# An attention and token/channel-mixer kernel: plain loads and casts for the first q and k halves, all run-time masks on VectorE, gated v loads, and a listed order for the opening

## The chip, the cores and the metric

The kernel runs on one core of one Trainium2 chip. The metric is the device time of one execution in microseconds (us); lower is better. Engines are called PE (TensorE matmul), PEld (its weight loads), DVE (VectorE), ACT (ScalarE), POOL (GpSimd) and SP (SyncE, which here only issues DMAs).

## What is computed

Four batches of eight heads go through causal attention with a window of 128 positions and four sink positions; the result goes through a token mixer and a channel mixer. Cut to what matters, with B, H, S, D = 4, 8, 768, 64:

```python
scores = (q @ k.T) / sqrt(D)                       # per head, 768 x 768
keep   = (pos_k < 4) | ((0 <= pos_q - pos_k) & (pos_q - pos_k < 128))
a      = softmax(where(keep, scores, -1e9))
x      = (a @ v), heads side by side               # 4 x 768 x 512
h      = relu(x.T @ w_tok1) @ w_tok2               # w_tok1 768 x 256, w_tok2 256 x 768
u      = x + h.T
out    = u + relu(u @ w_ch1) @ w_ch2               # w_ch1 512 x 1536, w_ch2 1536 x 512
```

## The kernel before

Heads are taken in eight groups of four, two groups to a batch. Work is written as operations with names: a prefix, the group or batch, and an index. The names matter, because the change lists them.

Attention for group g: `Lq`, `Lk` load q and k as bf16; `Tq`, `Tk` turn them by 32x32 blocks on DVE (L354); `KZ` makes a block form of the four sink keys (L378). Scores are made transposed, keys on the partitions, and only where the window allows: key tile kt meets query tiles kt and kt+1. `SCg.u` covers key tiles 2u and 2u+1 (u = 0, 1, 2) for four heads (L406); groups 0 and 1 split it into two pairs of heads. `EX` takes the exponential from PSUM to SBUF as tile pT (ACT, L423). `MK` zeroes what the window excludes (below). `SK` and `EXK` do the sink scores (L476, L481). `PVg.qt` multiplies by v for one query tile (L495, L498, L503); v carries a column of ones, so the last column is the sum. `XB` divides by it into the batch's x (DVE, L518, L519). `Lv` loads v as float32 through SP (L335) and `Cv` casts it (L211 on DVE or L212 on POOL).

Mixer for batch b: `T1` (L547) and `H1` (relu), then `T2` (L599), `U` (add x, DVE L604), `X` (transposes, L609) and `UTE` (copies). Batch 0 makes part of this directly as `TT` (L578, L581) and `UE`. Then `C1` (L632) with its relu `V` (ACT L217 or DVE L219), `C2` in three parts (L654), `O` (residual add, DVE L664) and `ST` (store, SP L669). Weights `Wtok1`, `Wtok2`, four pieces `Wch1` and two `Wch2` are float32 in HBM and are cast by DMAs that POOL issues (L714), as are q and k (L325).

Masks before: DVE multiplies pT by a 0/1 tile for the first half of u = 0 (`MKg.0h`, 1024 elements per partition, L444). All other 128-wide blocks (512 elements over the four heads) are separate operations that may go to POOL as affine selects (L224, L229) or to DVE as multiplications (L437). For two score blocks, (1,1) and (1,2), PE adds a mask of large negative numbers before the exponential instead (L399, from tile `mneg`).

The order is decided when the program is built. `order_of` is a greedy list planner: each operation has a cost per engine, a priority and, for loads, a landing time; at each step it takes the operation that can start first, by priority and distance from the end within 0.2 us. Each engine then runs its own list strictly in order and waits for semaphores of the others. PSUM is planned as slots: two of kind `sc` (two banks each, scores) and four of kind `mx` (one bank each, everything else). Where the plan sees PE idle before 36 us, `Filler` puts dummy matmuls on a zero tile `warm` there (L754); they depend on the memset of `warm` alone (L233). The planner starts PE at 0.8 us and does not add that memset to a filler's start.

v loads: five of them stand at the head of SP's list and wait for nothing on other engines, since the raw tiles have five buffers. SP's plain loads and POOL's casting loads are two DMA queues.

Of the kernel before, what the change touches and what calls it, by code (L numbers as in the profile page):

```python
# [9 lines left out]
FP32 = mybir.dt.float32  # L10
# [4 lines left out]

INF = float("inf")


# [7 lines left out]
class Op:  # L26
# [4 lines left out]
    def __init__(self, name, engines, emit, deps=(), pri=0, rows=False, take=(), free=(), land=0.0, dear=None):  # L31
        self.name, self.engines, self.emit = name, engines, emit
        self.deps, self.pri, self.rows = [d for d in deps if d is not None], pri, rows
        self.take, self.free, self.land, self.dear = take, free, land, dear or {}
        self.dmas = 1 if land else 0
        self.far = 0.0
        self.begin = self.end = self.engine = None
        Op.n += 1
        self.seq = Op.n
# [11 lines left out]
def order_of(ops, slots, filler):  # L51

    free_at = {e: 0.8 for e in ("PE", "ACT", "DVE", "POOL", "SP")}
    banks = {kind: [0.0] * n for kind, n in slots.items()}
    dma_free, rows = 1.9, False
    flying = {"SP": [0.0] * 8, "POOL": [0.0] * 8}
# [21 lines left out]
    while waiting:  # L78
# [30 lines left out]
        if o.land:  # L109
            dma_free = max(dma_free, t + 1.2) + o.land  # L110
            o.end = dma_free + 0.9
            flying[e] += [o.end] * o.dmas
        else:
            o.end = free_at[e]
# [21 lines left out]
def kernel(  # L136
# [34 lines left out]
    singles = ctx.enter_context(tc.tile_pool(name="singles", bufs=1))  # L171
    stage = ctx.enter_context(tc.tile_pool(name="stage", bufs=5))
    bfp = ctx.enter_context(tc.tile_pool(name="bfp", bufs=2))
# [15 lines left out]
    mfirst = singles.tile([P, 2 * P], BF16, name="mfirst")  # L189
    mrest = singles.tile([P, 2 * P], BF16, name="mrest")  # L190
    mneg = singles.tile([P, 2, 4 * P], BF16, name="mneg")
# [113 lines left out]
    groups = [Group() for _ in range(NG)]  # L305
    PEM = ((1, 1), (1, 2))
    PIECES = (2, 1, 1, 1, 1, 1, 1, 1)
    PAIRS = (1,)
    V0, V0w = 1, "q"
    BW, BWV = 0.37, 0.25  # L310

    def load_ops(g, deps, vdeps, pri):

        G = groups[g]
        C = PIECES[g]
        R = S // Q // C
        G.bf, G.load = {}, {"q": [], "k": [], "v": []}
        prev = groups[g - 2] if g >= 2 else None
        pieces = [(w, c) for c in range(C) for w in "qk"]
        for n, (w, c) in enumerate(pieces):  # L320
            def emit(e, w=w, c=c):
                if w not in G.bf:
                    G.bf[w] = bfp.tile([P, S // Q, D], BF16, name=w + "b")
                src = heads(q if w == "q" else k, g)
                nc.gpsimd.dma_start(out=G.bf[w][:, ts(c, R)],  # L325
                                    in_=src.rearrange("h (i r) d -> (h i) r d", i=Q)[:, ts(c, R)])
            o = op(f"L{w}{g}.{c}", ("POOL", 0.8), emit, deps + (prev.dt[w] if prev else []), pri + n,
                   land=GH * S * D * 4e-6 / BW / C)
            G.load[w].append(o)
        parts = 2 if g == 1 else 1  # L330
        for x in range(parts):
            def vv(_, x=x, n=GH // parts):
                if "v" not in G.bf:
                    G.bf["v"] = stage.tile([P, GH * S * D // P], FP32, name="raw_v", tag="raw")
                nc.sync.dma_start(out=G.bf["v"].rearrange("p (n d) -> p n d", d=D)[:, ds(x * n * NT, n * NT)],  # L335
                                  in_=heads(v, g)[ds(x * n, n)].rearrange("h (t p) d -> p (h t) d", p=P))
            G.load["v"].append(op(f"Lv{g}.{x}", ("SP", 0.46), vv, vdeps, pri + 2, land=GH * S * D * 4e-6 / BWV / parts))


    def attention(g, xb, base):  # L340
# [31 lines left out]
        veng = {"POOL": 1.02e-3 * N}  # L372
        if g < 2:
            veng |= {"DVE": dve(N, 2), "ACT": act(N)}
        G.cv = [op(f"Cv{g}", veng, castv, G.load["v"] + [c_va_op] + old, -5 if g < 2 else base + 2)]
# [51 lines left out]
        def masks(u, ex):  # L427
            if (g, u) in PEM:
                return []
            n = 512 if u < 2 else 384  # L430

            def block(e, x, c):
                t = G.pT[u][:, :, ds(256 * x + P * c, P)]
                if e == "POOL":
                    (causal, behind)[c](nc.gpsimd, t, 0.0)
                else:
                    nc.vector.tensor_tensor(  # L437
                        out=t, in0=t, op=ALU.mult,
                        in1=mrest[:, ts(c, P)].rearrange("p (o x) -> p o x", o=1).to_broadcast([P, GH, P]))
            r, xs = [], [0, 1]  # L440
            if u == 0:
                def head(e):
                    t = G.pT[u][:, :, 0:2 * P]
                    nc.vector.tensor_tensor(  # L444
                        out=t, in0=t, op=ALU.mult,
                        in1=mfirst[:, 0:2 * P].rearrange("p (o x) -> p o x", o=1).to_broadcast([P, GH, 2 * P]))
                r = [op(f"MK{g}.0h", ("DVE", dve(1024, 2)), head, ex + [c_first_op], base + u)]
                xs = [1]
            for x in xs:
                for c in range(2 if 2 * u + x < NT - 1 else 1):  # L450
                    r.append(op(f"MK{g}.{u}{x}{c}", {"POOL": 0.76, "DVE": dve(512, 2) + 0.1}, lambda e, x=x, c=c: block(e, x, c),
                                ex + [c_rest_op], base + u, dear={"DVE": 0.6}))
            return r
# [248 lines left out]
    for o in groups[0].load["v"] + groups[1].load["v"]:  # L702
        o.deps += groups[V0].load[V0w][-1:]
    o_vsl = op("vsl", ("POOL", 2.6), c_vsink_load, [o_vs, groups[0].load["k"][1]], -150, land=0.2)
    o_vsl.dmas = 4
    c_vsink_op = op("vs1", ("POOL", 0.6), c_vsink_one, [o_vs, o_vsl], -60)
    o_first = op("first", ("POOL", 0.65), c_masks(mfirst), [o_ones], -120)
    c_first_op = op("first1", ("DVE", 0.17), c_mfirst_sink, [o_first], -120)
    c_rest_op = op("rest", ("POOL", 0.65), c_masks(mrest), [o_ones], -20)

    def weight(key, dst, src, deps, pri, run):

        def emit(e):
            nc.gpsimd.dma_start(out=dst, in_=src)  # L714
        w_ops[key] = op(f"W{key}", ("POOL", 0.8), emit, deps, pri, land=dst.shape[0] * dst.shape[1] / 16 * run * 1e-3)
        return w_ops[key]
# [14 lines left out]
    for b in range(B):  # L731
        batches[b].x = X(batches[b - 2].u if b >= 2 else [])
        for a in range(GB):
            g = GB * b + a
            if g >= 2:
                deps = [c1w[3]] if g < 4 else []
                load_ops(g, deps, deps + groups[g - 2].cv, 1000 * b - 700)
            attention(g, batches[b].x, 1000 * b + 10 * a)
        mixer(b, 1000 * b + 50, 1000 * b + 1100)
    for o in ops:  # L740
        if 0 <= o.pri < 60:
            o.pri = 0

    class Filler:
# [48 lines left out]
```

## Time and profile before

| what | value |
|---|---|
| median of 6 runs | 221.9 us (221.14 to 222.26) |
| the profiled execution's own time | 221.65 us |
| its span, first to last instruction | 219.7 us |
| what lies around the span | 1.95 us |
| mean granted TensorE clock | 0.999 |
| PE busy | 204.3 us, 93% of the span |
| DVE busy | 122.0 us, 56% |
| ACT busy | 104.3 us, 47% |
| POOL busy | 65.6 us, 30% |
| DMA | 23.10 MB, mean 105 GB/s |

PE is the busiest engine by far, so the table is read for where PE is not busy: the first 33 us, a stretch between 77 and 110 us, and the tail. In the timeline a line gives the start, the duration, the engine, the source line, the operation, its tiles, and in brackets the idle time of that engine just before and what ended it. In the chain of work that ended last, a line gives a start, a duration and what held the end of the kernel at that moment. A DMA's packets are counted in the bytes that they write, so a casting load of 384 KB has read 768 KB.

### The profile page before, as it was taken

What the parts mean: (1) busy time and instruction counts of PE and PEld (TensorE: products, weight loads), DVE (VectorE), ACT (ScalarE), POOL (GpSimd) and SP (SyncE); (2) the same over time, 40 slices, a digit from 0 to 9 for tenths busy, and PEclk for the clock granted to TensorE, in tenths of its full rate; (3) what the DMA queues carried; (4) which work ended last, traced back from release to release, by engine and by line L of the source; (5) the groups of instructions that cost most, each with busy time, mean ns of one, the idle gap of its engine ahead of it and who ended that gap; (6) DMA issues with size and microseconds to landing.
All of it is one profiled execution on the core that took longest, in us unless ns stands there. A gap on an engine that the chain in (4) does not pass through costs nothing.

```text
span 219.7 us, 4249 instructions
## 1 busy us (share of the span) xinstructions
PE 204.3 (93%) x1767; PEld 115.7 (53%) x1767; DVE 122.0 (56%) x222; ACT 104.3 (47%) x174; POOL 65.6 (30%) x105
## 2 busy tenths in 40 slices
PE   7976799999999967899999999999999999999993
PEld 3332486555545635467555554467655545655552
DVE  6769972091778999999994113578481122001131
ACT  2077516753347676684565330587553301753300
POOL 7919940006038889562020000146100000000000
PEclk9999999999999999999999999999999999999999
DMA  7999999998999898320000112200001112101122
GB/s 149 223 213 221 208 204 206 211 213 177 233 215 218 198 213 139 36 46 0 3 0 0 51 48 95 97 3 3 0 0 51 48 48 104 43 1 48 48 97 97
DMA packets 36243, 23.10 MB, mean 105 GB/s; under 512 B 26112, under 2 KB 31488, under 8 KB 36224
## 3 DMA queue, kind: packets, MB, share of 16 engines
q0 software_dynamic: 7904, 10.24, 27.8%
q1 hardware_dynamic: 28320, 12.59, 23.5%
q8 instruction: 14, 0.23, 0.4%
q14 instruction: 5, 0.04, 0.1%
HBM read 26.77 MB, written 6.29 MB: 150 GB/s over the span
## 4 chain that ended last, share of the span: by engine, by line
PE 77%; DMA 7%; DVE 6%; POOL 4%; ACT 2%; issue 1%; POOLq 0%; ACTq 0%
PE ps_v L632 29%; PE ps_w L654 28%; PE ps_u L599 5%; DMA w_tok<-in_moe_w_tok_dram 4%; PE ps_h L547 4%; DMA vsink<-in_v_dram 3%; PE ps_s L406 3%; PE ps_ut L609 2%; PE ps_o L498 2%; DVE kT L354 2%; PE ps_o L503 2%; PE ps_o L495 2%; ACT pT L423 1%; PE ps_k L476 1%; DVE pT L444 1%
## 5 line engine op out<-in xcount | busy, mean ns | idle before, releaser
L217 ACT ACTIVATE v<-ps_v 128x384 bf16<-128x384 f32 x90 | 44.2, 491 | 53.4 <-PE ps_v L632 42.2
L632 PE MATMUL ps_v<-uT,w_ch 128*128 128x384 bf16 x384 | 67.4, 326 | 0.2
L654 PE MATMUL ps_w<-w_ch,v 128*128 128x512 bf16 (+1 forms) x300 | 65.0, 371 | 0.0
L423 ACT ACTIVATE pT<-ps_s 128x1024 bf16<-128x1024 f32 (+1 forms) x48 | 43.3, 952 | 36.4 <-PE ps_s L406 33.9
L664 DVE TENSOR_TENSOR o<-ps_w,u_sb 128x512 f32<-128x512 f32 (+1 forms) x25 | 16.7, 669 | 67.6 <-PE ps_w L654 67.6
L632 PEld LDWEIGHTS <-w_ch 128*128 128x128 bf16 x384 | 36.5, 98 | 25.3 <-DVE x_b L519 0.6
L654 PEld LDWEIGHTS <-v 128*128 128x128 bf16 x300 | 29.1, 98 | 31.3 <-issue 0.2
L224 POOL TENSOR_SCALAR_AFFINE_SELECT pT<-pT 128x512 bf16<-128x512 bf16 x29 | 21.9, 761 | 54.6 <-issue 32.4
L604 DVE TENSOR_TENSOR u_sb<-ps_u,x_b 128x512 bf16<-128x512 f32 x24 | 15.3, 682 | 12.5 <-PE ps_u L599 12.4
L519 DVE TENSOR_TENSOR x_b<-ps_o,rc 128x256 bf16<-128x256 f32 (+1 forms) x45 | 19.9, 442 | 1.6
L406 PE MATMUL ps_s<-qT,kT 32*128 32x256 bf16 (+1 forms) x384 | 16.9, 263 | 2.6 <-ACT pT L423 1.1
L354 DVE STREAM_TRANSPOSE qT<-qb 128x768 uint32<-128x768 uint32 (+1 forms) x9 | 16.8, 1865 | 3.6 <-DMA qb<-in_q_dram 3.6
L498 PE MATMUL ps_o<-va,pT 128*128 128x65 bf16 x192 | 15.8, 194 | 1.6 <-DVE pT L444 1.0
L354 DVE STREAM_TRANSPOSE kT<-kb 128x768 uint32<-128x768 uint32 (+1 forms) x9 | 16.9, 1872 | 0.2
L498 PEld LDWEIGHTS <-pT 128*128 128x128 bf16 x192 | 13.5, 98 | 4.4 <-DVE pT L444 1.3
L406 PEld LDWEIGHTS <-kT 32*128 32x128 bf16 x384 | 9.4, 92 | 11.6 <-issue 7.8
L503 PE MATMUL ps_o<-va,pT 128*128 128x65 bf16 x160 | 14.8, 193 | 0.0
L547 PE MATMUL ps_h<-x_b,w_tok 128*128 128x256 bf16 x96 | 12.3, 273 | 1.6 <-DMA w_tok<-in_moe_w_tok_dram 1.3
L599 PE MATMUL ps_u<-h,w_tok 128*128 128x512 bf16 x48 | 12.5, 378 | 1.3 <-DVE u_sb L604 0.9
L229 POOL TENSOR_SCALAR_AFFINE_SELECT pT<-pT 128x512 bf16<-128x512 bf16 x19 | 12.9, 685 | 0.0
L754 PE MATMUL ps_warm<-warm 128*128 128x512 bf16 x43 | 11.3, 423 | 1.3 <-DVE warm L233 1.3
L325 POOL DMA_DIRECT2D qb<-in_q_dram x9 | 5.0, 558 | 24.1 <-DVE qT L354 21.9
(61 smaller groups left out, 159.1 us busy)
## 6 DMA issues: line engine op xcount, KB each, us to landing
out_dram<-o SPq DMA_DIRECT2D x23, 256.0 KB, 2.0
raw_v<-in_v_dram SPq DMA_DIRECT2D x7, 768.0 KB, 8.3
qb<-in_q_dram POOLq DMA_DIRECT2D x7, 384.0 KB, 6.6
kb<-in_k_dram POOLq DMA_DIRECT2D x7, 384.0 KB, 7.9
w_ch<-in_moe_w_ch_dram POOLq DMA_DIRECT2D x4, 384.0 KB, 11.1
w_ch<-in_moe_w_ch_dram POOLq DMA_DIRECT2D x1, 1024.0 KB, 15.3
raw_v<-in_v_dram SPq DMA_DIRECT2D x2, 384.0 KB, 14.5
w_tok<-in_moe_w_tok_dram POOLq DMA_DIRECT2D x2, 384.0 KB, 8.2
```

The lines of the kernel that those rows point to most:

```text
L217: nc.scalar.activation(o, i, AF.Relu)
L224: eng.affine_select(out=t, in_=t, compare_op=ALU.is_ge, fill=fill, base=0, pattern=[[0, t.shape[1]], [1, P]], channel_multiplier=-1)
L354: nc.vector.transpose(G.T[w].rearrange("p s x -> p (s x)").bitcast(UINT32).rearrange("p (i r) -> p r i", i=Q)[:, r], G.bf[w][:, r].bitcast ...
L406: nc.tensor.matmul(bank[h][:, at:at + w], G.T["k"][r, ts(kt, P), db], G.T["q"][r, ds(kt * P, w), db], start=not pem and db == 0, stop=db = ...
L423: nc.scalar.activation(o, i, AF.Exp, scale=scale)
L498: nc.tensor.matmul(ps[:, h], G.pT[qt // 2][:, h, ds(256 * (qt % 2), P)], G.va[:, h, qt], start=(qt < 2 and h == 0), stop=(h == GH - 1 and ...
L503: nc.tensor.matmul(ps[:, h], G.pT[kt // 2][:, h, ds(256 * (kt % 2) + P, P)], G.va[:, h, kt], start=False, stop=(h == GH - 1), skip_group_c ...
L519: nc.vector.tensor_tensor(out=xb.tile[:, ds(q0, n), c0:c0 + W].rearrange("p n (h d) -> p n h d", h=GH), in0=ps[:, :, :, 0:D], in1=rc.to_br ...
L547: nc.tensor.matmul(p.tile, w_tok1[:, t, ts(tt, P)], xb.tile[:, t, ds(a * W, W)], start=(t == 0), stop=(t == NT - 1))
L599: nc.tensor.matmul(ps, w_tok2[:, tt, ts(st, P)], M.h1t[:, tt], start=(tt == 0), stop=(tt == NTOK - 1))
L632: nc.tensor.matmul(ps, w_ch1[:, c, ts(ft, P)], M.uT[hf][:, c], start=(c == 0), stop=(c == NC - 1))
L654: nc.tensor.matmul(p.tile, M.v1t[hf][:, ft, ts(st % NH, P)], w_ch2[:, ft, ds(lo, n)], start=(ft == 0), stop=(ft == NF - 1))
```

## The change

- For group 0 the first halves of q and k are loaded as float32 by SP (two plain DMAs at the head of its list, ahead of the v loads) and cast: k's by DVE, q's by ACT. The other halves and all later q and k stay with POOL.
- POOL takes no masks at run time. `MK` is now on DVE alone, in larger pieces: for u = 0 two of 1024 elements (the mask tiles `mfirst` and `mrest`), for u = 1 one of 2048, for u = 2 one of 1536. `mrest` becomes 512 wide. Of the two blocks masked on PE only (1,2) stays; (1,1) becomes a DVE piece. The cast `Cv` of every group is now POOL's.
- The raw v tiles have three buffers instead of five, and the load of v for groups 2 and 3 carries a wait on one of the `Wch1` weight pieces, so what stands behind it on SP waits too.
- The planner counts the landing of SP's and POOL's DMAs apart and with other delays.
- A list `FIRST` gives the order and the engine of some 160 operations of groups 0 and 1 and of batch 0's first mixer part. Among other things it puts the memset of `vsink` (2080 elements, 1.8 us) ahead of that of `warm` on DVE, moves `mneg`'s selects on POOL behind the sink loads `vsl`, puts `Cv0` ahead of the weight DMAs and `Cv1` behind the first two, and takes the third score block of groups 0 and 1 first.
- After the opening the planner makes another order too. In the built program PE's scores of groups 4 and 5 now stand among `C1` of batch 1; before, those of groups 2 to 5 all stood among `C2` of batch 0 and the start of batch 1. PE has 38 fillers ahead of its first score instead of 35, and two more sets of three later.

The diff, cut to its core:

```diff
+FIRST = """
+MK0.00:D UE0.03:A PV1.3:P vs1:G XB0.1:D SK1:P C10.03:P C10.02:P Tq0.1:D Lv0.0:S Tk1.0:D PV1.5:P XB1.2:D
...
+"""
-    dma_free, rows = 1.9, False
+    dma_free, rows = {"SP": 1.9, "POOL": 3.4, "ACT": 1.9}, False
...
-            dma_free = max(dma_free, t + 1.2) + o.land
-            o.end = dma_free + 0.9
+            dma_free[e] = max(dma_free[e], t + (2.5 if e == "POOL" else 1.4)) + o.land
+            o.end = dma_free[e] + 0.9
...
-    stage = ctx.enter_context(tc.tile_pool(name="stage", bufs=5))
+    stage = ctx.enter_context(tc.tile_pool(name="stage", bufs=3))
...
-    mrest = singles.tile([P, 2 * P], BF16, name="mrest")
+    mrest = singles.tile([P, 4 * P], BF16, name="mrest")
...
-    PEM = ((1, 1), (1, 2))
+    PEM = ((1, 2),)
...
+            if g == 0 and c == 0:
+                def plain(e, w=w, src=src):
+                    raws[w] = stage.tile([P, R, D], FP32, name="raw_" + w, bufs=1)
+                    nc.sync.dma_start(out=raws[w], in_=src)
+
+                def cast(e, w=w, bf=bf):
+                    copy_on[e](bf(), raws[w])
+                o = op(f"L{w}{g}.{c}", ("SP", 0.46), plain, [], pri + n, land=land)
+                o = op(f"C{w}{g}.{c}", {"ACT": act(R * D), "DVE": dve(R * D, 2)}, cast, [o], pri)
+            else:
+                def casting(e, src=src, bf=bf):
+                    nc.gpsimd.dma_start(out=bf(), in_=src)
...
+                if gate:
+                    behind_of(ins, gate)
...
         veng = {"POOL": 1.02e-3 * N}
-        if g < 2:
-            veng |= {"DVE": dve(N, 2), "ACT": act(N)}
...
-            n = 512 if u < 2 else 384
-
-            def block(e, x, c):
...
+            for lo, hi, m in ((0, 256, mfirst), (256, 512, mrest)) if u == 0 else ((0, 512 if u == 1 else 384, mrest),):
+                def mask(e, lo=lo, hi=hi, m=m):
+                    t = G.pT[u][:, :, lo:hi]
+                    nc.vector.tensor_tensor(out=t, in0=t, op=ALU.mult,
+                                            in1=m[:, 0:hi - lo].rearrange("p (o x) -> p o x", o=1).to_broadcast([P, GH, hi - lo]))
+                r.append(op(f"MK{g}.{u}{lo}", ("DVE", dve(4 * (hi - lo), 2)), mask, ex + [c_first_op, c_rest_op], base + u))
...
-                load_ops(g, deps, deps + groups[g - 2].cv, 1000 * b - 700)
+                load_ops(g, deps, deps + groups[g - 2].cv, 1000 * b - 700, c1w[3] if g < 4 else None)
...
+    for n, word in enumerate(FIRST.split()):
+        name, e = word.split(":")
+        e = {"P": "PE", "A": "ACT", "D": "DVE", "G": "POOL", "S": "SP"}[e]
+        o = by_name[name]
+        o.pri, o.engines = n - 9999, {e: o.engines[e]}
```

The letters behind the names are engines: P for PE, A for ACT, D for DVE, G for POOL, S for SP.

## The prediction

> **What bounds it now.** I read the slices first, then the chain that ended last, then busy time by stretch, then single rows.
>
> ```profile
> PE   7976799999999967899999999999999999999993
> DVE  6769972091778999999994113578481122001131
> POOL 7919940006038889562020000146100000000000
> ```
>
> A slice is 5.5 us. PE is full except in slices 1 to 5, around 15 to 17, and at the end. DVE is full around slices 12 to 20, where PE dips. So there are two losses to explain: the opening, and the stretch around 77 us. The chain in order of time gives the first:
>
> ```profile
> 8.89 7.62 DMA vsink<-in_v_dram
> ...
> 17.56 0.54 POOL pT L229
> 18.10 0.59 POOL pT L224
> 18.70 0.56 POOL pT L229
> 19.25 8.08 DMA w_tok<-in_moe_w_tok_dram
> 27.33 0.05 issue
> 27.38 0.61 PE ps_h L547 x4
> ...
> 32.97 0.33 PE ps_ut L578 x2
> ```
>
> POOL waited for the small sink loads, then did three masks, and only then issued the first weight; that landed 8.1 us later, and PE, which works in order, stood until 27.38. TT begins at 32.97. I use that start as the end of the opening. Stretches give the second loss (length, then busy PE, PEld, DVE, ACT, POOL):
>
> ```profile
> 62.50:77.00 14.50, 14.50 (x190) 8.27 (x190) 12.08 (x28) 9.93 (x12) 10.63 (x13) 1.00 0.96 204
> 77.00:88.00 11.00, 7.80 (x131) 5.02 (x131) 10.72 (x15) 7.87 (x13) 9.54 (x15) 1.00 0.98 175
> 88.00:99.00 11.00, 9.94 (x141) 6.08 (x139) 10.47 (x27) 8.22 (x11) 6.81 (x10) 1.00 0.27 40
> 99.00:110.00 11.00, 10.09 (x118) 6.78 (x115) 10.63 (x23) 5.61 (x12) 1.38 (x2) 1.00 0.01 1
> ```
>
> PE loses 3.2, 1.1 and 0.9 us here, with DVE 95 to 97% busy: DVE is the bound. With 0.2 us after 110, PE's waits between TT and the tail are 5.4 us. All other time after 33 us is PE work, which the change does not alter.
>
> **Part 1, the opening, by my own walk through the new order with durations of these rows.**
>
> *Loads.* A 256 KB store lands in 2.0 us and a 128 KB one in 1.7. The plain 384 KB loads are larger and start beside nothing; I take 3.5 to 5.5 us (below, the stores' rate; above, the 5.3 to 7.2 us of the casting halves), so k lands near 4.7 and q near 6. The Trainium skill ("DMA: Bandwidth & Descriptors", section "Issuing engines are not separate DMA queues") speaks against a gain: all queues share the 16 engines, and another issuer saves only issue time. By it the four halves would be ready when they were, at 10.2. The trace for 6 to 8 us (packets, MB):
>
> ```profile
> q0 software_dynamic: 260, 0.36, 99.5%
> q1 hardware_dynamic: 262, 0.06, 17.2%
> ```
>
> The queues alternate packet by packet, so SP's 256-byte v packets lose to large ones, and a large-packet load in SP's queue gets a full share. I take a gain for q and k of about 1 us; it is worth nothing anyway, for the next reason.
>
> *Fillers.* These rows matter most:
>
> ```profile
> 1.26 9.26 PE L754 MATMUL ps_warm<-warm 128*128 128x512 bf16 x35 [1.26 <-DVE warm L233]
> 2.41 1.79 DVE L282 MEMSET vsink<- 128x2080 bf16 x1 [0.38 <-issue]
> ```
>
> Now `warm` comes after vsink 1.79, mneg 0.46, masks 0.80 and kz 0.31: from 0.93 to about 4.5 with its own 0.27. The 38 fillers start there: 8 at 0.425 us (the first 3.3 us in the trace), then 30 at 0.213: end 14.3. DVE has all four halves turned by 11.3 to 12.4 (cast 0.7, four times 1.13, the last POOL half landing at 9). So the first scores start at 14.3, not 11.43: 2.9 us later, by fillers.
>
> *From there ACT, then DVE.* ACT's twelve exponentials cost 0.9 us (1024) or 0.7 (768), the two sink ones 0.5. From 14.9: EX0 is done at 19.9, EXK0 20.4, EX1 (behind Tq1 at 19.6 and SK1) 20.85 to 26.65. DVE from 19.6: MK0 0.61+0.61+1.15, MK1 the same, six XB of 0.55 and three double ones of 0.85: 10.6 us from start to start, with 0.1 of gaps: XB1.4 ends at 30.3. T1's last four matmuls end at 30.85, against 32.97: 2.1 us sooner.
>
> *Is the weight there?* POOL: sink loads issued by 9, landed by 15 to 16.5 (before 16.5); `vs1` 0.9; Cv0 1.5; Wtok1 issued between 17.5 and 19.1. No v2 or v3 packets compete any more, so it moves at the 0.205 MB/us of the casting queue alone: 2.5 to start, 1.9, 2 to land, 24 to 26. T1 asks at 26.05: no wait, or half a us. Moving Cv0 ahead of it costs 1.5 us that the skipped masks (1.7 in the chain) pay for. Wch1 follows Cv1 (v1 lands at 18.7); its last piece lands at 34, asked for at 37; Wch2 at 42, asked for at 47. Covered.
>
> *Port.* The trace shows masks and POOL in each other's way:
>
> ```profile
> 84.20 1.47 POOL L212 CAST va<-raw_v 128x1536 bf16<-128x1536 f32 x1
> 84.23 1.99 DVE L444 TENSOR_TENSOR pT<-pT,mfirst 128x1024 bf16<-128x1024 bf16 x1
> ```
>
> Alone L444 takes 0.68. It took 1.11 at 22.77, beside weight issues. The Trainium skill ("SBUF — State Buffer", section "SBUF: two separate sides") says that a DVE operation with two SBUF inputs and a GpSimd one that reads SBUF take one port pair by exclusive lock. That speaks against putting all masks on DVE while POOL casts and issues: by the rule each of six opening masks could wait for a whole cast or issue, 0.9 us, 5 us in all. The rows give less: eight L444 have a median of 0.79, 0.1 over the clean value, with two bad ones. Bounds 0 and 5 us; I take 0.9 for the opening (about 0.15 per mask), which is near the median. Opening: 2.1 - 0.9 = 1.2 us gained.
>
> **Part 2, the middle.** Masks on DVE: from 512 at 0.43 and 1024 at 0.68, 1536 is 0.93 and 2048 is 1.18, so a group costs 0.68+0.68+0.93+1.18 = 3.5 us, four groups 13.9. Before, groups 2 to 5 paid 4.3 (L444: 0.69, 0.69, 1.99, 0.89) and 3.7 (L437). DVE gets 5.9 us more, in the stretch that it already bounds. Against that, the planner spreads groups 2 to 5 among more PE work: by the end of batch 2's `X`, eleven C1 (0.65) and three C2 parts (0.86), 9.8 us of PE, now come first.
>
> I walk it. SC2 starts at 30.85 + 24.8 = 55.6 (four C2 parts and two C1 fewer than before). From there to batch 1's last X, PE has 26.2 us and DVE 24.2 (masks 7, twelve XB at 0.55, five O and six U at 0.61, the rest 4). Waits of PE: 0.8 at SC2.1 and 0.45 at SC2.2, both for exponentials to free `sc` slots; masks keep up. From SC4: 0.15 for Tk4, 0.65 at SC4.2 for exponentials, 0.5 at PV4 for `mx` slots, 0.2 for a mask. `PV5.4` waits for MK5.2 behind Tq6, just covered by C1 and C2 parts; if that cover goes, 1 us. Sum 2.75, say 3.0. Cv5 at 66 can meet MK3 as in the row above, 1.3 us, part of it covered: 0.4. Middle: 3.4 instead of 5.4, gained 2.0; PE is set back by ACT and slots more than by masks.
>
> *The gate.* v2 waits for the third Wch1 piece, about 32. Queued behind it on SP: v3 to v6, then the first stores. v packets get one for one against weight packets of 1 KB (a weight slows by at most a fifth) and q, k packets of 3 KB (by 7%), so k3 lands at 50 to 52 (before 52; turned at 52, its first product at 58.8) and v2 at 52, v3 at 55, asked for at 58.5 and 67. Stores behind v6 land by 66; O0.4 asks for the buffer at 75. Free, with 6 us of cover for v2. After 110 us DVE has slack (13.3 of 22 us), so 3 us more masks for groups 6 and 7 cost nothing; price without that cover, 3.
>
> **Sum.** Opening 1.2 and middle 2.0: 3.2 off the profiled execution's 221.65 (span 219.7 and 1.95 around it) gives 218.45. The median stands 0.25 above that execution, so 218.7.
>
> **Rivals.**
> 1. *Both parts work undiminished* (0.22). No port loss, masks clean: 2.1 + 2.7 = 4.8, 217.1; to 215.8 if fillers end sooner. For it: POOL has far fewer operations than before. Against: its casts and issues remain just where masks stand.
> 2. *The gain is swallowed* (0.10). The late fillers and the port keep TT at 33, and the middle loses as much as before: 221 to 222.3. For it: the 2.9 us at the first scores are certain; L444 at 1.11.
> 3. *DVE becomes a harder bound in the middle: slower* (0.14). Place: SC4 to the last PV5, where by my list DVE holds 14.7 us and PE 13.6. If the 5.9 us are not spread, PE's waits rise from 5.4 to 11.3; less the opening's 1.2, that is 4.7 slower: 226.4. It decides once the middle's waits exceed 6.6 us. For it: DVE 97% busy. Against: the chain shows ping-pong with XB and U there, and C1 of batch 1 now stands between.
> 4. *The gate does harm*: k3 or v3 late by over 6 us; inside rival 3's range.
>
> **Numbers.** My forecast, 217.3 to 220.7, has 0.54. Below 217.3: 0.22; 220.7 to 222.6: 0.10; above: 0.14. From 215.8 to 221.8 leaves out about 0.03 below and 0.16 above. About 0.3% (0.7 us) is what a measurement of this kernel can tell from no change: faster 0.79, same 0.07, slower 0.14.
>
> **What will show it.** Fillers: PE's row of 38 begins at 4.5 and ends at 14.3, and the first L435 scores follow at once. TT near 31.8. The first weight issued by POOL between 17 and 19, and no long wait for it. Masks in the middle 0.7 and 1.2 us, a few with over 0.3 more beside a POOL cast. PE's waits from TT to 115 us between 2.7 and 4.5, named exponentials rather than masks. I am wrong if TT starts after 33, if PE waits for transposes of group 2, or if PE's middle waits pass 6.6.

## The result, and the profile after

The changed kernel takes 220.82 us (median of 35 runs, 218.72 to 221.75); the kernel before takes 222.0 beside it (72 runs, 221.14 to 223.93). The ratio is 0.9935, 95% interval 0.992 to 0.995: 1.4 us, or 0.65%, faster. The forecast was 3.2 us. The profiled execution takes 221.68 us with a span of 219.8 and a mean granted clock of 0.982, so it is one of the longer of the 35. Their times follow the granted clock: two runs at 1.0 take 218.7, about a dozen near 0.991 take 219.5 to 220.5, the rest near 0.982 take 220.6 to 221.75. (Where a kernel's runs below fall into groups over 1.5% apart, its ratio is of the quicker runs alone, which in e1 and e6 take in one of the slower group (218.7 and 219.9 us), so the median of all its runs is given too.)

The slices of the kernel after, with the granted clock:

```profile
PE   0995999999989999998999999999999999999993
DVE  7656796429939999999998912498755122001132
POOL 7919710002360212020200000000000000000000
PEclk9998599999999999999999999999999999999999
```

PE's dip around 77 us is nearly gone, as is POOL's work there. The opening holds three new things: PE is empty in slice 0, DVE is busy for 5 to 7 tenths of slices 2 to 4, where before it had 6, 9 and 9, and the clock is halved in slice 4. The chain that ended last names them (start, duration, what held the end):

```profile
4.75 0.28 DVE warm L247
5.07 11.07 PE ps_warm L773 x38
16.15 0.47 PE ps_s L435 x10
16.63 1.52 ACT pT L452 x2
18.18 3.30 DVE pT L463
21.48 0.11 DVE kz L407
21.64 1.03 PE ps_k L489 x2
22.67 0.96 PE ps_s L435 x7
23.64 1.39 PE ps_warm L773 x3
25.03 0.85 PE ps_k L489 x2
...
36.33 0.60 PE ps_h L560 x4
36.92 0.33 PE ps_ut L591 x2
```

The dummy matmuls hold the start until 16.1, then one mask until 21.5, then PE itself. TT begins at 36.92; before it was 32.97. The timeline of the kernel after shows what that mask stood beside:

```profile
16.19 1.46 POOL L226 CAST va<-raw_v 128x1536 bf16<-128x1536 f32 x1
17.59 1.59 POOL L727 DMA_DIRECT2D w_tok<-in_moe_w_tok_dram  x2
18.18 3.30 DVE L463 TENSOR_TENSOR pT<-pT,mrest 128x1536 bf16<-128x1536 bf16 x1 [4.31 <-ACT pT L452]
19.17 1.49 POOL L226 CAST va<-raw_v 128x1536 bf16<-128x1536 f32 x1
20.57 4.64 POOL L727 DMA_DIRECT2D w_ch<-in_moe_w_ch_dram  x6
...
69.28 0.96 DVE L463 TENSOR_TENSOR pT<-pT,mrest 128x1536 bf16<-128x1536 bf16 x1
```

A mask of 1536 elements takes 0.95 to 0.96 us in the middle of this kernel (last line). This one, the first of the opening (MK0.20), starts while POOL issues the first two weights, stays open through the whole of POOL's second v cast (Cv1) and ends at 21.48, 0.8 us after it. `KZ0` waits behind it on DVE, `SK0` waits 1.8 us for `KZ0`, and PE works in order, so it stands. What that does to the clock is seen per microsecond (length, busy PE, PEld, DVE, ACT, POOL, granted clock, DMA share, GB/s):

```profile
20.00:21.00 1.00, 0.00 (x0) 0.00 (x0) 1.00 (x1) 1.00 (x2) 1.00 (x2) 0.91 0.84 109
21.00:22.00 1.00, 0.36 (x1) 0.13 (x2) 1.00 (x3) 0.02 (x1) 1.00 (x2) 0.50 1.46 199
...
26.00:27.00 1.00, 1.00 (x20) 0.54 (x13) 0.00 (x0) 0.11 (x1) 0.31 (x1) 0.50 1.27 193
27.00:28.00 1.00, 1.00 (x22) 0.94 (x20) 0.28 (x2) 1.00 (x2) 0.00 (x0) 0.68 1.31 201
```

The clock column puts the half rate from 20.8 to 27.6 us: SK0 takes 1.03 us instead of 0.62, three dummies 1.46 instead of 0.82. A busy PE in these rows is a PE at half its rate.

The profile of the kernel before has no such spell, which is rare for it: of the 74 executions of it that stand beside the experiments, four kept a granted clock of 1.0. But a spell cost it little: these four took 221.7 us on average, the 38 at 0.992 took 222.0. In the kernel after, the two runs at 1.0 are some 1.3 us quicker than those at 0.992 and 2.5 quicker than those at 0.982.

The middle in the stretches that the prediction showed:

```profile
66.00:77.00 11.00, 10.36 (x146) 6.14 (x148) 10.36 (x24) 7.02 (x9) 1.47 (x1) 1.00 1.09 238
77.00:88.00 11.00, 11.00 (x114) 6.68 (x106) 10.19 (x20) 2.88 (x5) 2.01 (x2) 1.00 0.41 104
88.00:99.00 11.00, 10.76 (x94) 5.87 (x92) 10.66 (x15) 7.13 (x12) 1.59 (x3) 1.00 0.52 101
99.00:110.00 11.00, 10.18 (x165) 6.86 (x165) 10.24 (x24) 10.12 (x17) 1.47 (x1) 1.00 0.33 53
```

PE now loses 0.64, 0, 0.24 and 0.82 here, with 0.63 in 55 to 66 and 0.24 after 154: 2.6 us instead of 5.4. So the opening lost 3.95 us and the rest, from TT to the end, won 3.85 (182.9 against 186.7). A small result is the sum of two large ones.

### The profile page after: what moved, and what is told of

Read it like the earlier page. It is cut to its first block, busy times and chain, and to the rows that moved or that the text cites. A ratio compares the mean times of both kernels' runs of the same rounds, so it can differ in the third digit from the quotient of the medians.

```text
span 219.8 us, 4168 instructions
## 1 busy us (share of the span) xinstructions
PE 206.5 (94%) x1764; PEld 116.5 (53%) x1764; DVE 133.0 (60%) x232; ACT 101.6 (46%) x170; POOL 34.2 (16%) x57
## 4 chain that ended last, share of the span: by engine, by line
PE 88%; DVE 7%; ACT 3%; issue 1%; DVEq 0%
PE ps_w L667 28%; PE ps_v L645 28%; PE ps_s L435 6%; PE ps_warm L773 6%; PE ps_u L612 5%; PE ps_h L560 4%; DVE pT L463 3%; PE ps_o L511 3%; ACT pT L452 2%; PE ps_o L516 2%; PE ps_o L508 2%; PE ps_ut L622 2%; PE ps_k L489 2%; DVE vsink L296 1%; PE ps_ut L591 1%
## 5 line engine op out<-in xcount | busy, mean ns | idle before, releaser
L667 PE MATMUL ps_w<-w_ch,v 128*128 128x512 bf16 (+1 forms) x300 | 66.1, 371 | 0.0
L231 ACT ACTIVATE v<-ps_v 128x384 bf16<-128x384 f32 x86 | 42.1, 493 | 45.0 <-PE ps_v L645 33.9
L463 DVE TENSOR_TENSOR pT<-pT,mrest 128x1024 bf16<-128x1024 bf16 (+2 forms) x23 | 24.2, 1053 | 4.9 <-ACT pT L452 4.6
L435 PE MATMUL ps_s<-qT,kT 32*128 32x256 bf16 (+1 forms) x384 | 18.2, 272 | 1.5 <-ACT pT L452 1.4
L226 POOL CAST va<-raw_v 128x1536 bf16<-128x1536 f32 x8 | 11.8, 1475 | 49.1 <-DMA raw_v<-in_v_dram 25.0
L773 PE MATMUL ps_warm<-warm 128*128 128x512 bf16 x44 | 13.4, 469 | 5.1 <-DVE warm L247 5.1
L511 PE MATMUL ps_o<-va,pT 128*128 128x65 bf16 x192 | 16.6, 196 | 0.7 <-DVE h L233 0.3
L435 PEld LDWEIGHTS <-kT 32*128 32x128 bf16 x384 | 9.9, 94 | 11.7 <-issue 10.3
L511 PEld LDWEIGHTS <-pT 128*128 128x128 bf16 x192 | 13.9, 99 | 3.0 <-DVE h L233 0.6
L516 PE MATMUL ps_o<-va,pT 128*128 128x65 bf16 x160 | 15.0, 195 | 0.0
L227 ACT ACTIVATE uT<-ps_ut 128x512 bf16<-128x512 bf16 (+1 forms) x13 | 7.3, 564 | 13.0 <-PE ps_ut L622 12.6
```

The lines of the kernel that those rows point to most:

```text
L231: nc.scalar.activation(o, i, AF.Relu)
L435: nc.tensor.matmul(bank[h][:, at:at + w], G.T["k"][r, ts(kt, P), db], G.T["q"][r, ds(kt * P, w), db], start=not pem and db == 0, stop=db = ...
L463: nc.vector.tensor_tensor(out=t, in0=t, op=ALU.mult, in1=m[:, 0:hi - lo].rearrange("p (o x) -> p o x", o=1).to_broadcast([P, GH, hi - lo]))
L511: nc.tensor.matmul(ps[:, h], G.pT[qt // 2][:, h, ds(256 * (qt % 2), P)], G.va[:, h, qt], start=(qt < 2 and h == 0), stop=(h == GH - 1 and ...
L667: nc.tensor.matmul(p.tile, M.v1t[hf][:, ft, ts(st % NH, P)], w_ch2[:, ft, ds(lo, n)], start=(ft == 0), stop=(ft == NF - 1))
L773: nc.tensor.matmul(t, warm[:, 0:P], warm, start=True, stop=True)
```

## The experiments

The theory (A): the middle won as forecast or better; the opening lost because `warm`'s memset, now seventh on DVE, delays the whole row of dummies and with it the first scores, so that the opening masks meet POOL's cast, the stall lowers the clock, and PE runs at half rate. The rivals were that the load order, the gate or the masks of the middle lost it. The table gives for each kernel where PE's row of the first TT product (the timeline's start, a little earlier than the chain's) divides its profiled span; "rest" is the span behind it. The edits are cut to their core.

| kernel | median of all runs, us | ratio to before (95%) | first scores | TT | rest |
|---|---|---|---|---|---|
| before | 222.0 | 1 | 11.43 | 32.80 | 186.9 |
| after | 220.82 | 0.9935 (0.992 to 0.995) | 16.08 | 36.76 | 183.0 |
| warm first (e1) | 219.04 | 0.9785 (0.972 to 0.985), 3 quickest | 12.43 | 30.92 | 183.1 |
| second v cast late (e2) | 219.44 | 0.9881 (0.9852 to 0.9909) | 16.05 | 34.93 | 183.1 |
| gap filled (e3) | 219.01 | 0.9866 (0.9841 to 0.9892) | 16.01 | 34.76 | 183.0 |
| e1 and e2 together (e4) | 216.04 | 0.9733 (0.9707 to 0.9759) | 11.51 | 30.41 | 183.7 |
| later masks as before (e5) | 222.4 | 1.0013 (0.9995 to 1.0031) | 16.05 | 36.77 | 183.9 |
| no gate (e6) | 220.2 | 0.9818 (0.9763 to 0.9874), quickest | 15.04 | 31.77 | 183.6 |
| before, later masks on DVE (e7) | 221.62 | 0.9966 (0.994 to 0.9992) | 11.64 | 33.21 | 185.9 |
| no list (e8) | 222.62 | 1.0041 (1.0017 to 1.0065) | 11.14 | 32.30 | 188.4 |
| short row of dummies (e9) | 217.33 | 0.9712 (0.9669 to 0.9755), quickest | 11.49 | 28.54 | 184.3 |
| before, warm late (e10) | 222.92 | 1.0048 (1.0027 to 1.007) | 13.65 | 34.20 | 186.9 |
| e4 without gate (e11) | 217.37 | 0.98 (0.9773 to 0.9828) | 12.35 | 30.77 | 184.9 |
| e4, later masks as before (e12) | 222.92 | 1.0047 (1.0025 to 1.0069) | 11.64 | 30.48 | 190.4 |
| short row, cast late (e13) | 215.79 | 0.9721 (0.9691 to 0.975) | 11.59 | 30.23 | 183.5 |

**The opening: dummies, cast and clock**

`warm` alone moved back to the head of DVE's order:

```diff
+        line = order_of(ops, slots, Filler)
+        line.remove(o_warm)
+        line.insert(0, o_warm)
```

> The changed kernel with one operation moved: the memset of warm is the first on DVE instead of the seventh; all other orders are the same. Theory A (the opening is lost to late fillers, then to a mask that GpSimd holds up, then to a TensorE clock at half rate): fillers start at 1.6 instead of 5.07 and end by 11 to 13, the first scores follow at 12 to 13 instead of 16.1, the first mask meets GpSimd while it waits for the sink loads and takes about 1 us instead of 3.3, the key block is there before SK0 asks, and TT starts at 33 to 34.5 instead of 36.9; time 217.5 to 219.0, and the granted clock nearer to 1. Rival B (the opening hangs on loads, casts and weights, and the fillers only fill a gap): first scores earlier but TT within 0.7 us of 36.9 and the time within 0.7 us of the changed kernel's 220.8.

First scores came 3.65 us earlier and TT 5.8 earlier, with the rest of the span unchanged. But the six runs are 215.8, 215.9, 218.7, 219.3, 219.6 and 220.2: the race is still on. Even the profiled run, one of the quick ones, shows it: MK0.20 is clean, and a later mask is held through the same cast, which ended at 20.60. The clock falls here too, from 17.3 to 20.7 us, though no single wait of PE before it was over 0.41 us.

```profile
14.53 0.96 DVE L463 TENSOR_TENSOR pT<-pT,mrest 128x1536 bf16<-128x1536 bf16 x1 [0.79 <-ACT pT L452]
18.06 3.10 DVE L463 TENSOR_TENSOR pT<-pT,mrest 128x1024 bf16<-128x1024 bf16 x1
```

`Cv1` alone moved behind the first three of POOL's six `w_ch` issues:

```diff
+        cv1 = by_name["Cv1"]
+        line.remove(cv1)
+        line.insert(line.index(by_name["Wch1.3"]) + 1, cv1)
```

> The changed kernel with one operation moved on GpSimd: the cast of group 1's v (Cv1) stands behind three weight issues instead of ahead of all four. Theory A: the mask that took 3.3 us from 18.2 was held by the casts on GpSimd; without Cv1 there it takes 1 to 2 us, SK0 starts 1.2 to 2.3 us sooner, the clock falls later or not at all, TT starts 1 to 3 us sooner; time 218.3 to 220.0. If descriptor writing for weights holds the mask just as a cast does, the mask stays above 2.5 us and the time at 220.8. Rival B: no change of the time, 220.8 within 0.7.

```profile
18.16 0.96 DVE L463 TENSOR_TENSOR pT<-pT,mrest 128x1536 bf16<-128x1536 bf16 x1 [4.23 <-ACT pT L452]
19.03 1.45 DVE L407 TENSOR_TENSOR kz<-kT,blk 128x32 bf16<-128x32 bf16 x1
20.54 0.86 PE L489 MATMUL ps_k<-qT,kz 128*128 128x512 bf16 x2 [0.69 <-DVE kz L407]
```

At the same place in time, the same mask takes 0.96 us when POOL issues weights in place of casting: without the cast behind them, the `w_tok` issues do not hold it. But a hold is left: `KZ0`, right behind the mask and clean at 0.18 us in the kernel after, takes 1.45 beside the first `w_ch` issues (19.12 on). So SK0 starts 1.1 us sooner, not 2.3, and still waits 0.69. The half-rate spell comes all the same but is half as long, 3.4 us (20.8 to 24.2) instead of 6.8. TT comes 1.8 us earlier.

Work added, nothing taken away: eight more dummies ahead of `SK0`.

```diff
+        f = Filler.make("mx", 3, 8)
+        f.engine = "PE"
+        line.insert(line.index(by_name["SK0"]), f)
```

> The changed kernel with eight more dummy matmuls ahead of SK0, where TensorE stood 1.8 us; no wait is taken away. Theory A, the part about the clock: TensorE stays busy through the gap, the granted clock stays at 1, the scores, sink scores and products from 21.6 to 27.4 run at full rate, and TT starts 1.5 to 3 us sooner; time 218.7 to 219.8 although work is only added. Rival C (the half clock hides behind ACT and DVE, which set the pace there anyway): time unchanged within 0.5 of 220.8, or up to 0.5 slower.

```profile
18.11 3.39 DVE L463 TENSOR_TENSOR pT<-pT,mrest 128x1536 bf16<-128x1536 bf16 x1 [4.25 <-ACT pT L452]
...
19.74 1.90 PE L773 MATMUL ps_warm<-warm 128*128 128x512 bf16 x8
21.66 0.62 PE L489 MATMUL ps_k<-qT,kz 128*128 128x512 bf16 x2
```

The mask is held as long as ever and SK0 starts at 21.66 as against 21.64, but at full rate; every run shows a clock of 0.999 or 1.0. TT comes 2.0 us earlier, and the median falls by 1.8. That is the price of the half clock by itself; the two runs of the kernel after that kept their clock by chance, 218.7 us, agree with e3's 219.0.

The first two edits together, so that `warm` stands first and `Cv1` behind `Wch1.3`:

> Both moves: warm first on DVE and Cv1 behind three weight issues. Theory A: as with warm first alone, 217.3 to 218.8, and another 0 to 1 us less where later masks met Cv1; TT at 32.5 to 34. Rival B: 220.8 within 0.7. If warm first alone already takes the mask out of GpSimd's way, the second move adds nothing, and Cv1 may now be late for PV1.0, which asks for it about 27 to 30: up to 0.5 us lost.

```profile
13.71 0.95 DVE L463 TENSOR_TENSOR pT<-pT,mrest 128x1536 bf16<-128x1536 bf16 x1
16.55 1.64 DVE L463 TENSOR_TENSOR pT<-pT,mfirst 128x1024 bf16<-128x1024 bf16 x1
18.72 2.48 DVE L463 TENSOR_TENSOR pT<-pT,mrest 128x2048 bf16<-128x2048 bf16 x1
```

Five runs lie between 215.8 and 216.5: steady, 4.8 us below the changed kernel. Two masks are still long, by 1.0 us (beside POOL's first cast, 16.19 to 17.65) and by 1.26 us (beside weight issues, no cast near), and a third loses 0.6 us beside the second cast, at its new place, so issues can hold a mask too, as they held `KZ0` in e2, by as much. PE's waits for masks here sum to 1.0 us.

`warm` left late, but 16 dummies where the planner put 38:

```diff
-            for _ in range(n):
+            for _ in range(16 if n == 38 else n):
```

> The changed kernel, with 16 dummy matmuls instead of 38 ahead of the first scores; warm stays behind vsink on DVE. Theory A (it is the length of the filler row from its late start that sets the first scores, and their lateness that puts MK0.20 beside POOL's second v cast): fillers 5.1 to about 11.6, first scores at 11.6 to 12.0 (q and k are turned at 11.55), MK0.20 0.95 to 1.0 us, TT near 31, and 216 to 219 us with two clusters, as with warm first. Rival (the early filler start matters by itself, for the clock: a short row leaves PE less busy before the scores): the granted clock falls below 0.9 between 12 and 27 us, and the time stays at 219.5 to 221.

```profile
5.07 6.23 PE L773 MATMUL ps_warm<-warm 128*128 128x512 bf16 x16 [5.07 <-DVE warm L247]
11.49 0.55 PE L435 MATMUL ps_s<-qT,kT 32*128 32x256 bf16 x16 [0.19 <-DVE qT L385]
```

The first scores start when q is turned, at 11.5, with `warm` at its late place: what did the harm is a row that long from that start, not the want of an early start. The profiled run has a clock of 0.998, so the rival is out for the quick runs; for the slow ones (0.974 to 0.982) the next kernel decides. Runs split again: 214.6, 215.7 and 215.9 against 218.8, 218.8 and 219.6. In the quickest, DVE won the race and it was POOL's cast that grew, from 1.47 to 2.09 us. Moving that cast as well tells whether the race splits them:

```diff
-            for _ in range(n):
+            for _ in range(16 if n == 38 else n):
...
+        cv1 = by_name["Cv1"]
+        line.remove(cv1)
+        line.insert(line.index(by_name["Wch1.3"]) + 1, cv1)
```

> The changed kernel with 16 dummy matmuls instead of 38 ahead of the first scores (first scores at 11.5, 217.33 us, in two clusters near 215 and 219) and with POOL's second v cast moved behind the six issues of the w_ch pieces. Theory A (the slow cluster of the short row is the race of the opening masks against that cast): one cluster, all within 1 us, at 215 to 216.5, first scores at 11.5, as with warm first. Rival (the clusters come from the TensorE clock after a shorter warm-up): still two clusters, 3 us or more apart, and the slow runs at a lower granted clock.

(Here too the cast stands behind the first three of the six issues.) Six runs, 215.6 to 216.6, with clocks of 0.99 to 1.0 after the same short row: one group. Theory A holds, the rival does not, and this kernel and e4 are the best of all tried, equal within their intervals.

The same delay put into the kernel before (its `warm` behind `mneg`, `kz` and `vsink`):

```diff
+        for o in (o_zero, c_kz_op, o_vs):
+            line.remove(o)
+            line.insert(line.index(o_warm), o)
```

> The kernel before, with the memset of warm moved behind those of mneg, kz and vsink on DVE, and nothing else. Theory A: its 35 fillers start near 4.5 instead of 1.26 and end near 14.5, first scores 3 us later than 11.43; 1.3 us of that vanish in the wait for the first weight (PE's only long wait before TT), so TT at 34.5 to 35 and the whole 1.5 to 2.5 us slower than before: 223.5 to 224.5. Rival (the start of the opening has slack in the old order, POOL's masks and weights set TT): TT within 0.4 us of 33, time within 0.7 us of before.

The dummies run from 4.26 to 13.7, the first scores are 2.2 us late, TT 1.4 us late, and the median is 1.15 us higher: slower, by less than I had put. The first weight's wait of 1.3 us vanished as expected. The clock fell in the profiled run:

```profile
18.00:19.00 1.00, 1.00 (x10) 0.42 (x8) 1.00 (x2) 0.79 (x2) 1.00 (x3) 0.52 1.33 225
19.00:20.00 1.00, 1.00 (x7) 0.38 (x4) 1.00 (x1) 0.82 (x2) 1.00 (x3) 0.50 1.21 197
```

That is no mark of the late start, though: in e7 below, whose opening is that of the kernel before, it fell too (16.6 to 20.0), and e10's clocks over all runs (0.989 to 1.0) are no lower than those of the kernel before.

**The middle: masks, plan, list and gate**

Masks of groups 2 to 7 back to the old small pieces on POOL and DVE, in the changed kernel:

```diff
+            if g >= 2:
+                n = 512 if u < 2 else 384
+                def block(e, x, c):
...
+                return r
             r = []
             for lo, hi, m in ((0, 256, mfirst), (256, 512, mrest)) if u == 0 else ((0, 512 if u == 1 else 384, mrest),):
```

> The changed kernel, but the masks of groups 2 to 7 are again the old ones, in blocks that may go to GpSimd; the opening's order is untouched (TT at 36 to 37). Theory M1 (the middle gained because masks left GpSimd, which also sets the pace of casts and holds DVE up): TensorE's waits between TT and 115 us return from 2.6 towards 5.4 and the time rises by 1.5 to 3 us, to 222.3 to 223.8. Theory M2 (the middle gained because the new plan spreads groups 2 to 5 among channel-mixer work; who does the masks is second): the waits stay under 4 and the time within 1 us of 220.8.

Opening the same to 0.01 us, rest 0.9 us longer, median 1.6 higher. Neither theory has it whole: the time lies at the lower edge of M1, but PE's waits from TT on are 2.8 us against 2.6, as M2 said. The other way round, the new masks in the kernel before:

```diff
-    mrest = singles.tile([P, 2 * P], BF16, name="mrest")
+    mrest = singles.tile([P, 4 * P], BF16, name="mrest")
...
+            if g >= 2:
+                r = []
+                for lo, hi, m in ((0, 256, mfirst), (256, 512, mrest)) if u == 0 else ((0, 512 if u == 1 else 384, mrest),):
...
+                return r
```

> The kernel before with one part of the change: the masks of groups 2 to 7 on DVE in large pieces; opening, loads and buffers as before (TT at 33). M1: the middle gains what it gained in the changed kernel, 2.5 to 3.9 us; time 218 to 219.5. M2: with the old plan's crowding of groups 2 to 5, 5.9 us more DVE work makes the middle worse: 223 to 226, unless the planner reorders by itself, which in the built program it does in part (C1 of batch 1 now stands among groups 4 and 5): then 219.5 to 222.

Rest 1.0 us shorter, median 0.34% (0.75 us) lower by the ratio. So in either plan the masks' move is worth about 1 us of the rest, out of the 3.85 won. What is left, some 2.9 us, I put down to the plan's new order, by subtraction: no run changes that order alone. Then the same edit as e5 in the steady kernel e4:

> The changed kernel with warm first and POOL's second v cast late (216.0 us), and the masks of groups 2 to 7 as before (first blocks on DVE, the rest on POOL or DVE as the planner puts them). The opening is then steady, so this prices the masks' move alone. If DVE's relief from small pieces is worth what the undone masks cost in the disturbed kernel: 0.9 to 1.6 us slower, 216.9 to 217.6, PE waiting for POOL masks between 66 and 110 us. If the price there was only the clusters of the opening: within 0.4 us, 215.7 to 216.4.

This came out at neither figure: 6.9 us slower than e4. The waits of PE from 58 to 66 us, and the stretch behind:

```profile
PE ps_o L536 <- POOL pT L238: 4.4, 1, 4.4
```

```profile
62.00:63.00 1.00, 0.00 (x0) 0.00 (x0) 0.00 (x0) 0.00 (x0) 1.00 (x3) 0.90 1.08 223
63.00:64.00 1.00, 0.00 (x0) 0.00 (x0) 0.00 (x0) 0.00 (x0) 1.00 (x3) 0.50 1.28 242
...
69.00:70.00 1.00, 1.00 (x17) 0.82 (x16) 1.00 (x1) 0.00 (x0) 0.21 (x1) 0.68 1.08 265
```

With the opening six us earlier, the first mask of group 2 on POOL stands behind a v cast, which itself waits 2.1 us for a product of PE to free its buffer and starts at 60.16, and behind four load issues (61.57 to 63.66). PE waits 4.4 us, and in the empty stretch its clock halves, from 62.8 until 69.6. In e5 the late opening had covered this. Keeping masks off POOL is worth about 1 us where POOL has time and 6.9 us where it has none.

The list (it names 127 operations) emptied:

```diff
-FIRST = """
-MK0.00:D UE0.03:A PV1.3:P vs1:G XB0.1:D SK1:P C10.03:P C10.02:P Tq0.1:D Lv0.0:S Tk1.0:D PV1.5:P XB1.2:D
...
-"""
+FIRST = ""
```

> The changed kernel with an empty list: the planner orders the opening by its own priorities; warm is then first on DVE. Theory A: fillers start at 1.3, no long wait of TensorE before the weights; TT 33 to 35.5, time 218 to 220.5, below the changed kernel's 220.8. Rival B (the list is what the change gains by): TT after 37 and time over 221.5.

```profile
37.13 0.17 PE ps_ut L583 x3
...
60.83 7.43 DMA qb<-in_q_dram
```

Without the list the first TT product starts at 32.30, but that start misleads here: the four parts of TT, which follow each other at once in the kernel after, are spread, and the last ends at 37.3 against 38.9 (its chain has `38.73 0.17 PE ps_ut L594 x3`). By that end the opening is 1.6 us shorter, with a half-rate spell of 10.2 us in it, and the rest 2.5 us longer, with a chain that runs through a late q load: the list loses in the opening and wins behind it. By the time (222.6) it is rival B that came true, though not at the place that it named.

The gate removed, with five raw v buffers:

```diff
-    stage = ctx.enter_context(tc.tile_pool(name="stage", bufs=3))
+    stage = ctx.enter_context(tc.tile_pool(name="stage", bufs=5))
...
-                load_ops(g, deps, deps + groups[g - 2].cv, 1000 * b - 700, c1w[3] if g < 4 else None)
+                load_ops(g, deps, deps + groups[g - 2].cv, 1000 * b - 700)
```

> The changed kernel without the wait of v2 and v3 on a weight, and with five raw v buffers again; the orders of TensorE are the same. If the gate gives what the prediction said (no v packets beside the first weights: w_tok1 there by 24 to 26): w_tok1 lands 1 to 3 us later, about 25 to 26; with T1 asking for it at 32.6 this is covered, so the time is unchanged within 0.5 of 220.8. Rival: the gate is what keeps q and k of groups 2 and 3 in time or late; then the time moves by over 1 us, up or down.

Inconclusive by itself: the six runs, 216.9 to 221.6, split like those of the changed kernel, and in the profiled one the opening had got by with a mask of 1.38 us. The same edit in the steady e4:

> The changed kernel with warm first and POOL's second v cast behind the weights (216.0 us), and now without the gate on the v loads of groups 2 and 3, with five raw v buffers. PE's order is the same. Theory A and the forecast (the gate costs nothing and gives little, since weights land in time either way): 215.5 to 216.6. Rival (the gate was what makes the weights land in time): w_tok1 lands over 3 us later, T1 waits for it, 218 or more. Other rival (the gate delays something): below 215.3.

```profile
PE ps_w L667 <- DMA w_ch<-in_moe_w_ch_dram: 0.9, 1, 0.9
PE ps_v L645 <- DMA w_ch<-in_moe_w_ch_dram: 0.4, 1, 0.4
```

1.3 us slower than e4 (with the five buffers, which came back in the same edit), and these two waits between 33 and 56 us, which e4 doesn't have, are that 1.3. The four `w_ch` pieces landed 13.9 us after issue (median) instead of 9.7, w_tok 8.0 instead of 5.7. The gate gives what neither I nor the expectation had put on it, though not at the place that the rival named.

The first halves of q and k by casting loads again, in e4:

```diff
-            if g == 0 and c == 0:
+            if False:
```

The list's words for them change with it: `Lq0.0:S` and `Lk0.0:S` become `:G`, `Cq0.0:A` and `Ck0.0:D` go.

> The changed kernel with warm first and POOL's second v cast late (216.0 us), with the first halves of q and k loaded by POOL's casting DMAs again, as before the change; the two casts on ACT and DVE fall away. The planner makes another order after the opening, so the span's total is not read for this part, only the opening. The forecast (plain loads are worth nothing, as the second halves come last): q and k turned at 11.5 to 12.0, first scores within 0.3 us of 11.5, TT at 30 to 31. Rival (two loads fewer in the casting queue bring the second halves forward): all four halves about 2 us later, first scores at 13 to 14, TT at 32 or later.

Inconclusive: 230.78 us (ratio 1.0383, 1.0352 to 1.0415). The planner now put 55 dummies ahead of the first scores (to 15.93), and the order of the list, made for two loads fewer, let group 1's k go ahead of group 0's second halves, which were turned at 13.8 and 14.9 instead of 11.5. That says that this list needs the plain loads. It doesn't say what they are worth with four casting loads at the head of POOL's queue, where the kernel before had turned all four by 11.4.

## Why the prediction was wrong

The direction was right, but the gain was 1.4 us instead of 3.2, and the time, 220.8, lies just above the forecast's 217.3 to 220.7 (within the wide 215.8 to 221.8). What failed is Part 1: the opening was to gain 1.2 us and lost 3.95. That the total came out only 2.1 us from the forecast is luck, since the middle won nearly twice its share. By its own steps:

- **Fillers: right in kind, 1.8 us too short.** "8 at 0.425 us, then 30 at 0.213: end 14.3" ended at 16.1. The start was 5.07 instead of 4.5, and the slow phase was longer: 38 matmuls in 11.07 us are 14 at 0.425 and 24 at 0.213, 6.0 us of half rate. I had taken the 3.3 us of one execution for a constant. With 16 dummies the same late start cost nothing (e9, e13).
- **Port: this step failed.** "About 0.15 per mask, 0.9 for the opening" came from the median of eight rows. All but one of the masks up to 33 us were clean (0.68 to 0.72 for 1024, 1.23 for 2048), and one lost 2.35 us, in the chain. The rule of the Trainium skill that I weighed and discounted ("SBUF — State Buffer", "SBUF: two separate sides": whoever starts first holds the pair for its whole instruction, the other stands) speaks of losses of a whole instruction, which the average hid, but it does not fit this row as recorded: the mask began 0.99 us before Cv1 (1.49 us) and would have been done at 19.13, just as the cast began; it ended about its clean length after the cast instead. In e9 masks stood 1.06 us and 0.45 us ahead of that cast and were clean (0.68 for 1024, 1.21 for 2048), and the cast took 2.09; in e1 a mask 1.05 us ahead of it lost 2.4 us. So who wins is open. Weight issues, which I had put under the same rule although it speaks of operations that read SBUF, held a two-input DVE operation by 1.26 us in e2, e4, e11 and e13. What counts is which operation meets which, and my own walk had placed the masks there: a meeting cost nothing, or about what the other had left, or, in the long rows (2.35 to 2.4 us in the kernel after, e1 and e3), more than the whole cast.
- **Clock: missing from the sum.** No step or rival had it. It cost 2.0 us (e3). The Trainium skill ("TensorE: Matmul & The Clock Gate", "What's actually happening") says that PE falls to half clock after an idle window of about 3.4 us and needs as much sustained work to return. The traces agree in the half and in the length: a spell at half rate lasted 3.4 us (e1, e2, e7, e10), 6.8 (the kernel after, e5, e12) or 10.2 (e8), once, twice or three times 3.41, though PE was busy for most of it. They don't agree on what sets one off. Only e12 has an idle stretch longer than the page's window (4.4 us). In the kernel after PE was busy 0.98, 0.76, 0.63 and 0.00 us in the four microseconds from 17 to 21; in e1 no wait before the fall was over 0.41 us; and the kernel before stood 1.40 us ahead of its `SK` at 19.89 and kept its clock. By the page this stall, 1.8 us in SK0's row, would not have been a risk. The runs show that filling it kept the clock up (e3, six of six runs); which stall lowers it and which doesn't is open.
- Together: TT was put at 31.8 and came at 36.9. Of the 5.1 us, 1.8 is the fillers and 2.0 the clock; the 1.3 left is close to the port's excess, 2.35 less 0.9.
- **Weight: right.** It was issued at 17.6 and landed 5 to 6 us later, and nobody waited for it. **q and k**: turned by 11.55, as forecast; whether the plain loads were needed for that stays open (e14).
- **Middle: right in kind, mis-sized.** Forecast gain 2.0, measured 3.85. PE's waits were 2.6 instead of my 3.4, named exponentials more than masks as forecast. The waits explain 2.75 of it; some 1.1 us of PE's own time is left, which no run here explains, and matmul ends in these records are modelled. MK3 beside Cv5 took 1.35 us, as foreseen.
- **Gate: right that it costs nothing, and its gain not priced.** With the opening mended it is 1.3 us (e11); in this kernel e6 could not price it.
- **Rivals.** By its number the result falls at the edge of rival 2, which happened in its first half: TT was not held at 33 but pushed to 37. What made the kernel faster all the same was the middle, by twice what I had given it. Rival 3, DVE as a harder bound, did not appear: e5 and e12 show the opposite sign.

## What to carry to other kernels

A row of warm-up matmuls is a job with a length: when its start moves, its end moves, and the real work behind it, in order, pays; cap it by when the data arrive (16 in place of 38 dummies, with one cast moved, was worth 5 us here). Where operations of two engines hold each other up, don't average past collisions: list which operation will stand beside which, and price each meeting at both ends, nothing and a loss of the size of the other's operation (2.4 us at worst here). And a short stall of TensorE can cost its own length again in the clock (1.8 us of stall, 2.0 of clock); dummy matmuls that only fill a wait repaid it (e3). Last, a cover that hides a wait today (POOL's masks, the late weights) shows its price once the part before it is mended.

## What was not expected of the hardware

- The half-rate phase of the first dummies differs from execution to execution, whatever their start: worked out from the row's length as above, 3.6 us in the kernel before, 3.3 in e4, 4.0 in e10, 5.7 in e9, 6.0 in the kernel after and 6.1 in e11. The profile shows a granted clock of 1.00 in all of them during that time.
- Adding eight matmuls to the critical engine made the kernel 1.8 us faster.
- Weight issues by POOL held the DVE operation that stood beside the first `w_ch` issue by 1.26 us in all four kernels with the late cast (a 2048-element mask, 2.48 instead of 1.21 to 1.22 us, in e4, e11 and e13; `KZ0`, 1.45 instead of 0.19, in e2). Beside the `w_tok` issues (0.96 for 1536 elements in e2) and beside `w_ch` issues that follow a cast (0.72 and 1.23 in the kernel after, 1.21 in e1) masks were clean. Why is open.
